# Retention with a squared-ReLU layer on one core: tail stores as single transfers, seven products for the last group, another formula for S2 and later places for four loads

## The chip, the cores and the metric

The kernel runs on one core of one Trainium2 chip. The time is the device time of one launch in microseconds (us). A profile is one execution under the hardware profiler; its span, from first to last instruction, is about 2 us shorter than the time. With a single core there is no second die to compare with.

## The reference, cut to what matters

Eight batches of 576 positions and eight heads go through causal retention, and the result (4608 tokens of 512) through two dense layers with a squared ReLU between them.

```python
def _attn_ref(q, k, v):                        # [8, 8, 576, 64] each
    scores = scale * np.matmul(q, k.transpose(0, 1, 3, 2))
    ...
    Dmat = np.where(rel >= 0, gamma[:, None, None] ** rel[None, :, :], 0.0)
    return np.matmul(scores * Dmat[None], v)

def _moe_ref(x, w_in, w_out):                  # [4608, 512], [512, 2048], [2048, 512]
    r = np.maximum(x @ w_in, 0.0)
    return (r * r) @ w_out
```

576 is 4 x 128 + 64. The work is cut into units of 128 tokens: 32 full ones, and four "tail" units, each made of the last 64 positions of two batches. Two units are a group.

## The kernel before

A small scheduler in the program knows a duration and a wished place for every instruction, and from these it fixes the order on each engine. TensorE computes the first layer of a group (ph), ScalarE takes relu (rl), ScalarE or VectorE squares it (gT), and TensorE computes the second layer (po). From a certain group on the second layer uses seven products of quarter size in Strassen's way (Winograd's form). They need four sums S1 to S4 of quarters of gT (tile gS, on VectorE), each made in two halves:

```python
        s3 = add_sum(2, base - 12, lambda h: G(0, 0, h), lambda h: G(1, 0, h), ALU.subtract, low)
        s1 = add_sum(0, base, lambda h: G(1, 0, h), lambda h: G(1, 1, h), ALU.add, ...)
        s2 = add_sum(1, base + 1, lambda h: Sx(0, h), lambda h: G(0, 0, h), ALU.subtract, lambda h: [s1[h]])
        s4 = add_sum(3, base + 4, lambda h: G(0, 1, h), lambda h: Sx(1, h), ALU.subtract, lambda h: [s2[h]])
        ...
        p6 = product(6, 8, "a", summed(1), wT[1], lambda h: [s2[h]], False, True, [c1])
```

Only the last group (a tail unit and a full unit) is excepted and uses the plain second layer; its last unit is cut into two halves of columns. The result goes out with one function. A tail unit's tile holds 64 rows of one batch and 64 of the next, which lie apart in DRAM, so it takes two transfers:

```python
    def store(u, o, lo=0, hi=DM):
        kind, b, c = units[u]
        eng = nc.scalar if group_of[u] == len(groups) - 1 else nc.sync
        if kind == "full":
            r0 = b * S + c * P
            eng.dma_start(out=out[r0:r0 + P, lo:hi], in_=o[:, lo:hi])
        else:
            for i in range(2):
                r0 = (b + i) * S + 512
                eng.dma_start(out=out[r0:r0 + 64, lo:hi], in_=o[i * 64:(i + 1) * 64, lo:hi])
```

All loads are issued by SyncE in a fixed sequence, and the scheduler has one figure for when each lands:

```python
    FIRST = ["k0", "q0", "v0", "k2", "q2", "w0", "v2", "w1", "w2", ..., "k4", "q4", "v4", ...]
    ...
        t = dma_task(0, 2.75, fn, acq=("wst",))          # weights
```

## Time and profile before

| | before |
|---|---|
| time, median of 3 runs | 298.6 us (298.57 to 298.71) |
| span of the profile | 296.6 us |
| last matmul ends | 293.46 us |
| last store is issued | 293.88 us, 2.7 us before the span's end |

The second is the end of the same kernel in stretches of 1 us. The columns are the stretch, its length, five engines' busy time, TensorE's clock, the DMA engines' busy share and GB/s.

```profile
293.00:294.00 1.00, 0.45 (x5) 0.15 (x2) 0.00 (x0) 0.37 (x1) 0.00 (x0) 1.00 0.42 141
294.00:295.00 1.00, 0.00 (x0) 0.00 (x0) 0.00 (x0) 0.00 (x0) 0.00 (x0) 1.00 0.25 86
295.00:296.00 1.00, 0.00 (x0) 0.00 (x0) 0.00 (x0) 0.00 (x0) 0.00 (x0) 1.00 0.14 45
```

Within 2 us of the last matmul the bytes are out. (The 0.14 of the last line is one short burst: in quarters of a microsecond it is 0.55 and then three times 0.00.) The third is SyncE's queue in the middle, by start, duration of the issue, and transfer: a tail store as two transfers, and the loads of a full unit behind it.

```profile
166.31 1.18 SPq L796 DMA_DIRECT2D out_dram<-o  x2
167.53 0.58 SPq L277 DMA_DIRECT2D k<-in_k_dram  x1
168.16 0.69 SPq L277 DMA_DIRECT2D q<-in_q_dram  x1
168.90 0.83 SPq L277 DMA_DIRECT2D v<-in_v_dram  x1
```

The issue of a load takes 0.6 to 0.8 us behind this store, and 0.4 to 0.9 us from here to 180. That is the yardstick for the kernel after.

### The profile page before, as it was taken

The page shows a single profiled execution, that of the slowest core. Times are in us where ns is not written, and L with a number is a line of the kernel's source. Part 1 is how long each engine was busy: PE and PEld are TensorE (multiplying, and loading weights), DVE is VectorE, ACT ScalarE, POOL GpSimd, SP SyncE. Part 2 cuts the span into 40 slices and gives each one's busy share as a digit, 9 for nine tenths or more (in the row PEclk, how much of TensorE's full clock was granted, in tenths as well). Part 3 has the DMA queues.
Part 4 walks back from the last instruction along what each step waited for, and adds up shares of the span by engine and source line. Part 5 has one row for each costly group of instructions (what it writes and reads, how often), then busy time and mean ns, then how long its engine had stood idle before and what let it go on. Part 6 is the DMA issues. An engine that isn't in the chain of part 4 may idle for free.

```text
span 296.6 us, 10048 instructions
## 1 busy us (share of the span) xinstructions
PE 286.1 (96%) x4320; PEld 233.5 (79%) x4320; DVE 196.2 (66%) x413; ACT 187.5 (63%) x354; POOL 93.9 (32%) x129
## 2 busy tenths in 40 slices
PE   8979999999989999999999999999999999999995
PEld 3558755688878888888788888788888888888874
DVE  4777469967495959593959596766786766462410
ACT  5257753474867676648576667756666666658861
POOL 4454384544232506062414142435141520000000
PEclk9999999999999999999999999999999999999999
DMA  7999998899999989999969698999898980101012
GB/s 205 326 373 385 361 270 220 207 202 180 200 148 216 195 195 169 212 196 199 180 163 160 157 190 206 206 201 205 142 215 140 219 133 32 73 3 71 2 71 73
DMA packets 139261, 54.14 MB, mean 183 GB/s; under 512 B 118096, under 2 KB 130640, under 8 KB 139216
## 3 DMA queue, kind: packets, MB, share of 16 engines
q1 hardware_dynamic: 138768, 52.97, 86.2%
q8 instruction: 34, 0.56, 0.8%
q10 hardware_dynamic: 448, 0.52, 0.6%
q14 instruction: 11, 0.09, 0.1%
HBM read 36.70 MB, written 9.44 MB: 156 GB/s over the span
## 4 chain that ended last, share of the span: by engine, by line
PE 64%; DVE 11%; ACT 10%; DMA 9%; issue 2%; POOL 2%; POOLq 0%
PE po L912 26%; PE ph L819 25%; DVE gS L890 5%; ACT rl L827 5%; ACT gT L837 4%; PE psO L337 4%; PE po L860 4%; DMA pair<-in_v_dram 3%; DMA wo<-in_moe_w_out_dram 3%; DMA pair<-in_k_dram 3%; PE warm L241 2%; DVE gT L839 2%; PE psc L337 1%; PE psS L337 1%; PE psT L412 1%
## 5 line engine op out<-in xcount | busy, mean ns | idle before, releaser
L819 PE MATMUL ph<-xT,w_in 128*128 128x256 f16 x1152 | 139.3, 273 | 0.0
L819 PEld LDWEIGHTS <-w_in 128*128 128x128 f16 x1152 | 111.2, 98 | 14.8 <-POOL w_in L316 0.3
L827 ACT ACTIVATE rl<-ph 128x512 f16<-128x512 f32 x144 | 84.1, 588 | 51.4 <-PE ph L819 48.9
L837 ACT ACTIVATE gT<-rl 128x512 f16<-128x512 f16 x112 | 70.6, 630 | 3.4
L890 DVE TENSOR_TENSOR gS<-gT 128x512 f16<-128x512 f16 x60 | 31.8, 531 | 40.3 <-ACT gT L837 39.7
L912 PEld LDWEIGHTS <-gS 128*128 128x128 f16 x480 | 45.6, 98 | 9.8 <-DVE gS L890 4.5
L912 PE MATMUL po<-wT,gS 128*128 128x256 f16 x360 | 49.2, 273 | 2.0 <-DVE gS L890 1.9
L361 POOL TENSOR_TENSOR v<-v,vdec_full 128x512 f16<-128x512 f32 x24 | 26.2, 1092 | 58.4 <-DMA v<-in_v_dram 51.0
L912 PEld LDWEIGHTS <-gT 128*128 128x128 f16 x360 | 34.7, 98 | 4.2
L912 PE MATMUL po<-w_out,gT 128*128 128x256 f16 x240 | 31.1, 273 | 0.0
L349 POOL CAST kq<-k 128x512 f16<-128x512 f32 x28 | 19.0, 677 | 36.9 <-DMA k<-in_k_dram 35.6
L839 DVE TENSOR_TENSOR gT<-rl 128x512 f16<-128x512 f16 x32 | 18.1, 568 | 13.8 <-ACT rl L827 13.4
L349 POOL CAST kq<-q 128x512 f16<-128x512 f32 x28 | 18.1, 647 | 23.3 <-DMA q<-in_q_dram 23.2
L860 PE MATMUL po<-w_out,gT 128*128 128x512 f16 (+1 forms) x112 | 22.6, 349 | 0.1
L925 ACT COPY u<-po 128x256 f32<-128x256 f32 x30 | 11.0, 367 | 15.5 <-PE po L912 15.4
L935 DVE TENSOR_TENSOR o<-po,u 128x256 f32<-128x256 f32 x30 | 12.6, 419 | 11.8 <-PE po L912 8.1
L698 DVE TENSOR_TENSOR xT<-psO,gam_full 128x512 f16<-128x512 f32 x28 | 18.4, 684 | 2.7 <-PE psO L337 2.5
L637 DVE TENSOR_TENSOR rT<-psc,mask 128x512 f16<-128x512 f32 x28 | 18.5, 681 | 1.4 <-PE psc L337 1.4
L890 DVE TENSOR_TENSOR gS<-gS,gT 128x512 f16<-128x512 f16 x30 | 16.3, 544 | 1.0
L860 PEld LDWEIGHTS <-gT 128*128 128x128 f16 x112 | 10.6, 98 | 7.9 <-issue 0.2
L912 PE MATMUL po<-wT,gT 128*128 128x256 f16 x120 | 15.8, 273 | 0.0
L890 DVE TENSOR_TENSOR gS<-gT,gS 128x512 f16<-128x512 f16 x30 | 15.1, 505 | 1.0
(78 smaller groups left out, 264.2 us busy)
## 6 DMA issues: line engine op xcount, KB each, us to landing
out_dram<-o SPq DMA_DIRECT2D x31, 256.0 KB, 3.1
k<-in_k_dram SPq DMA_DIRECT2D x24, 256.0 KB, 4.9
q<-in_q_dram SPq DMA_DIRECT2D x24, 256.0 KB, 4.9
v<-in_v_dram SPq DMA_DIRECT2D x24, 256.0 KB, 4.6
wi<-in_moe_w_in_dram SPq DMA_DIRECT2D x4, 1024.0 KB, 9.9
wo<-in_moe_w_out_dram SPq DMA_DIRECT2D x4, 1024.0 KB, 9.5
pair<-in_k_dram SPq DMA_DIRECT2D x4, 512.0 KB, 5.7
pair<-in_q_dram SPq DMA_DIRECT2D x4, 512.0 KB, 5.4
```

The source lines that it names most:

```text
L337: nc.tensor.matmul(out_, lhsT=lhsT, rhs=rhs, start=start, stop=True, skip_group_check=True, tile_position=(64 * row, 64 * col))
L349: op(out=out_.rearrange("p (n b a d) -> p n b a d", n=2, b=2, a=2), in_=in_.rearrange("p (n a b) d -> p n b a d", n=2, a=2))
L361: nc.gpsimd.tensor_tensor(out=t, in0=tile_of["v32", u], in1=vdec[kind].rearrange("p (h o) -> p h o", o=1).to_broadcast([P, H, D]), op=ALU. ...
L637: nc.vector.tensor_tensor(out=r, in0=tile_of["psc", g][:, :, cols(s)].rearrange("p a (n i) -> p a n i", i=64), in1=mask.rearrange("p (o r ...
L698: nc.vector.tensor_tensor(out=tile_of["x", g][:, :, s * P:(s + 1) * P].rearrange("p n (c i) -> p c n i", c=2), in0=tile_of["psO", g][:, :, ...
L819: nc.tensor.matmul(tile_of["ph", g, fb][:, j, :], lhsT=w_in16[:, m, fi * P:(fi + 1) * P], rhs=tile_of["x", g][:, m, :], start=(m == 0), st ...
L827: nc.scalar.activation(out=t, in_=tile_of["ph", g, fb], func=ACTF.Relu)
L837: nc.scalar.activation(out=t, in_=rl, func=ACTF.Square)
L839: nc.vector.tensor_tensor(out=t, in0=rl, in1=rl, op=ALU.mult)
L860: nc.tensor.matmul(tile_of["po", u, lo], lhsT=tile_of["g", g][:, fi, s * P:(s + 1) * P], rhs=w_out16[:, fi, lo:hi], start=(fi == 0), stop= ...
L890: nc.vector.tensor_tensor(out=Sx(k, h), in0=in0(h), in1=in1(h), op=op)
L912: nc.tensor.matmul(tile_of["pb", g, bank], lhsT=left(i), rhs=right[:, i, :], start=(start and i == 0), stop=(i == HF - 1), skip_group_chec ...
```

## The change

The change has four parts. A tail unit is stored with one transfer instead of two, so that the queue holds fewer issues. The last group also gets seven products, with its first layer spread between the products of the group before, so that TensorE has fewer columns to do. S2 is taken as A22 - S3 instead of S1 - A11 (the two are equal), so that it no longer waits for S1. And the scheduler is told that four loads (v2, w1, k4, q4) come later, so that it places what depends on them later.

```diff
+    SPREAD = 0.9
+    SQ_LATE = (1, 4, 6)
+    LAG = {"v2": 1.2, "w1": 1.3, "k4": 0.7, "q4": 0.5}
...
-        t = dma_task(0, 2.75, fn, acq=("wst",))
+        t = dma_task(0, 2.75, fn, acq=("wst",), after=2.1 + LAG.get(f"w{i}", 0.0))
...
-    def store(u, o, lo=0, hi=DM):
+    def store(u, o, lo=0, hi=DM, eng=nc.sync):
...
-            for i in range(2):
-                r0 = (b + i) * S + 512
-                eng.dma_start(out=out[r0:r0 + 64, lo:hi], in_=o[i * 64:(i + 1) * 64, lo:hi])
+            eng.dma_start(out=out.rearrange("(b s) m -> b s m", s=S)[b:b + 2, 512:576, lo:hi], in_=o[:, lo:hi])
...
-        base = us[0] * L
+        base = min(us) * L
+        def place(x):
+            return base + x if g < last_g else base - NF * n - 1 + SPREAD * x
...
-        if STRASSEN <= g < len(groups) - 1:
+        if STRASSEN <= g:
             add_strassen(g, us, base2, sq)
...
-        s1 = add_sum(0, base, lambda h: G(1, 0, h), lambda h: G(1, 1, h), ALU.add, ...)
-        s2 = add_sum(1, base + 1, lambda h: Sx(0, h), lambda h: G(0, 0, h), ALU.subtract, lambda h: [s1[h]])
+        s2 = add_sum(1, base - 4, lambda h: G(1, 1, h), lambda h: Sx(2, h), ALU.subtract, lambda h: high(h) + [s3[h]])
+        s1 = add_sum(0, base + 1, lambda h: G(1, 0, h), lambda h: G(1, 1, h), ALU.add, ...)
...
+        if g == last_g:
+            ...                       # other PSUM banks for products 3 and 4, additions on VectorE
         for u, ds in ((uA, [d11, c12]), (uB, [d22, d21])):
-            st = add("SP", -0.5, 0.7, lambda u=u: store(u, o_tile(u)), deps=ds, after=2.5)
+            if g < last_g: ...        # as before
+            else: ...                 # last group: one store per half, on SyncE or ScalarE
```

More of the change, by code (lines that the diff above doesn't have):

```diff
@@ L292, in fn @@
             nc.sync.dma_start(out=x, in_=(k, q, v)[n][b, :, c * P:(c + 2) * P, :].rearrange("h (p e) d -> p h (e d)", e=2))
-        loaded[name, u] = loaded[name, u + 1] = dma_task(0, 1.81 if loaded else 2.9, fn, acq=("wst",) if name != "q" else ())
+        loaded[name, u] = loaded[name, u + 1] = dma_task(0, 1.81 if loaded else 2.9, fn, acq=("wst",) if name != "q" else (),
+                                                         after=2.1 + LAG.get(name + str(u), 0.0))
     def add_weight(i):
@@ L784 @@
     wT_done = t1 + t2 + t3 + t4
-    def store(u, o, lo=0, hi=DM):
+    def store(u, o, lo=0, hi=DM, eng=nc.sync):
         kind, b, c = units[u]
-        eng = nc.scalar if group_of[u] == len(groups) - 1 else nc.sync
         if kind == "full":
@@ L820, in f @@
                                          rhs=tile_of["x", g][:, m, :], start=(m == 0), stop=(m == NP - 1))
-                f1.append(add("PE", base + (nf * fb + j) * n, 0.01 + 0.2133 * n, f,
+                f1.append(add("PE", place((nf * fb + j) * n), 0.01 + 0.2133 * n, f,
                               deps=[T["x", u] for u in us] + wcast_of(nf * fb + j) + f1[-1:],
@@ L827, in fr @@
                 nc.scalar.activation(out=t, in_=tile_of["ph", g, fb], func=ACTF.Relu)
-            on_act = n == 2 and g >= STRASSEN and fb in SQ_ACT
+            on_act = g >= STRASSEN and fb in (SQ_ACT if g < last_g - 1 else SQ_LATE)
             def fg(fb=fb, on_act=on_act):
@@ L839, in fg @@
                     nc.vector.tensor_tensor(out=t, in0=rl, in1=rl, op=ALU.mult)
-            r = add("ACT", base + 4 * fb + 4, 0.6, fr, deps=[f1[-1]], acq=("rl",))
+            r = add("ACT", place(4 * fb + 4), 0.6, fr, deps=[f1[-1]], acq=("rl",))
             sched.free("ff", [r])
-            sq.append(add("ACT" if on_act else "DVE", base + 4 * fb + 6, 0.63 if on_act else 0.45, fg, deps=[r] + sq[:1],
+            sq.append(add("ACT" if on_act else "DVE", place(4 * fb + 6), 0.63 if on_act else 0.45, fg, deps=[r] + sq[:1],
                           acq=() if fb else ("g",)))
@@ L852, in add_ff @@
             f2 = T["ff2"][-1:] if s == 0 else f2[-1:]
-            cuts = [(0, DM)] if u != groups[-1][-1] else [(0, HM), (HM, DM)]
-            for ci, (lo, hi) in enumerate(cuts):
-                for fi in range(NF):
-                    def f(fi=fi, s=s, u=u, lo=lo, hi=hi):
-                        if fi == 0:
-                            tile_of["po", u, lo] = ps_ff.tile([P, hi - lo], FP32, name="po", tag="ff")
-                        nc.tensor.matmul(tile_of["po", u, lo], lhsT=tile_of["g", g][:, fi, s * P:(s + 1) * P],
-                                         rhs=w_out16[:, fi, lo:hi], start=(fi == 0), stop=(fi == NF - 1))
-                    f2.append(add("PE", base2 + NF * s + fi / len(cuts) + 8 * ci, 0.0025 + 0.2135 / len(cuts), f,
-                                  deps=[sq[fi // nf]] + wcast[4 + fi // 4] + f2[-1:],
-                                  acq=("ff",) if fi == 0 else ()))
-                def fo(u=u, lo=lo, hi=hi):
-                    if lo == 0:
-                        tile_of["o", u] = o_pool.tile([P, DM], FP32, name="o", tag="o")
-                    nc.scalar.copy(out=tile_of["o", u][:, lo:hi], in_=tile_of["po", u, lo])
-                oc = add("ACT", end + 1, 0.12 + 0.47 / len(cuts), fo, deps=[f2[-1]], acq=() if lo else ("o",))
-                sched.free("ff", [oc])
-                st = add(*(("ACT", end + 1.1, 0.05) if g == len(groups) - 1 else ("SP", -0.5, 0.7)),
-                         lambda u=u, lo=lo, hi=hi: store(u, tile_of["o", u], lo, hi), deps=[oc], after=2.5)
@@ new lines, in add_ff, with f @@
+            for fi in range(NF):
+                def f(fi=fi, s=s, u=u):
+                    if fi == 0:
+                        tile_of["po", u] = ps_ff.tile([P, DM], FP32, name="po", tag="ff")
+                    nc.tensor.matmul(tile_of["po", u], lhsT=tile_of["g", g][:, fi, s * P:(s + 1) * P],
+                                     rhs=w_out16[:, fi, :], start=(fi == 0), stop=(fi == NF - 1))
+                f2.append(add("PE", base2 + NF * s + fi, 0.216, f, deps=[sq[fi // nf]] + wcast[4 + fi // 4] + f2[-1:],
+                              acq=("ff",) if fi == 0 else ()))
@@ L874, in add_ff, with fo @@
+            def fo(u=u):
+                tile_of["o", u] = o_pool.tile([P, DM], FP32, name="o", tag="o")
+                nc.scalar.copy(out=tile_of["o", u], in_=tile_of["po", u])
+            oc = add("ACT", end + 1, 0.59, fo, deps=[f2[-1]], acq=("o",))
+            sched.free("ff", [oc])
+            st = add("SP", -0.5, 0.7, lambda u=u: store(u, tile_of["o", u]), deps=[oc], after=2.5)
             sched.free("o", [st])
@@ L899, in add_strassen @@
         s3[0]["acq"] = ("wst",)
-        s1 = add_sum(0, base, lambda h: G(1, 0, h), lambda h: G(1, 1, h), ALU.add, lambda h: low(h) + high(h) + s3[:1])
-        s2 = add_sum(1, base + 1, lambda h: Sx(0, h), lambda h: G(0, 0, h), ALU.subtract, lambda h: [s1[h]])
+        s2 = add_sum(1, base - 4, lambda h: G(1, 1, h), lambda h: Sx(2, h), ALU.subtract, lambda h: high(h) + [s3[h]])
+        s1 = add_sum(0, base + 1, lambda h: G(1, 0, h), lambda h: G(1, 1, h), ALU.add, lambda h: low(h) + high(h) + s3[:1])
         s4 = add_sum(3, base + 4, lambda h: G(0, 1, h), lambda h: Sx(1, h), ALU.subtract, lambda h: [s2[h]])
@@ L949, in add_strassen, with f7, f12 @@
         c4 = on_act_copy("u4", "a", 21, [p5])
-        d22 = on_dve_add(uB, 1, "c", "u4", 22, [p7, c4], ("o",))
-        sched.free("u4", [d22])
-        p3 = product(3, 20, "a", summed(3), wB[1, 1], lambda h: [s4[h]], False, True, [c4])
-        def f12():
-            nc.scalar.copy(out=o_tile(uA)[:, HM:], in_=bank("a"))
-        c12 = add("ACT", base + 25, 0.37, f12, deps=[p3, d11])
-        sched.free("ff", [c12])
-        p4 = product(4, 24, "c", raw(1, 1), wT[3], high, False, True, [d22])
-        d21 = on_dve_add(uB, 0, "c", "u2", 29, [p4, d22])
-        sched.free("ff", [d21])
-        sched.free("u2", [d21])
+        if g == last_g:
+            def f7():
+                t = tile_of["p1", g] = u_pool.tile([P, HM], FP32, name="p1", tag="p1")
+                nc.vector.tensor_tensor(out=t, in0=bank("c"), in1=tile_of["u2", g], op=ALU.add)
+            d7 = add("DVE", base + 18, 0.42, f7, deps=[p7, c2], acq=("p1",))
+            sched.free("u2", [d7])
+            d22 = on_dve_add(uB, 1, "c", "u4", 22, [c4, d7])
+            sched.free("ff", [d22])
+            sched.free("ff", [c4])
+            p3 = product(3, 20, "d", summed(3), wB[1, 1], lambda h: [s4[h]], True, True, [])
+            p4 = product(4, 24, "e", raw(1, 1), wT[3], high, True, True, [])
+            c12 = on_dve_add(uA, 1, "d", "u4", 25, [p3, d22])
+            d21 = on_dve_add(uB, 0, "e", "p1", 29, [p4, d22])
+            d22["acq"] = ("o",)
+        else:
+            d22 = on_dve_add(uB, 1, "c", "u4", 22, [p7, c4], ("o",))
+            sched.free("u4", [d22])
+            p3 = product(3, 20, "a", summed(3), wB[1, 1], lambda h: [s4[h]], False, True, [c4])
+            def f12():
+                nc.scalar.copy(out=o_tile(uA)[:, HM:], in_=bank("a"))
+            c12 = add("ACT", base + 25, 0.37, f12, deps=[p3, d11])
+            sched.free("ff", [c12])
+            p4 = product(4, 24, "c", raw(1, 1), wT[3], high, False, True, [d22])
+            d21 = on_dve_add(uB, 0, "c", "u2", 29, [p4, d22])
+            sched.free("ff", [d21])
+            sched.free("u2", [d21])
         sched.free("wst", [p3])
@@ L965, in add_strassen @@
         for u, ds in ((uA, [d11, c12]), (uB, [d22, d21])):
-            st = add("SP", -0.5, 0.7, lambda u=u: store(u, o_tile(u)), deps=ds, after=2.5)
-            sched.free("o", [st])
+            if g < last_g:
+                st = [add("SP", -0.5, 0.7, lambda u=u: store(u, o_tile(u)), deps=ds, after=2.5)]
+            else:
+                st = []
+                for d in ds:
+                    lo = 0 if d in (d11, d21) else HM
+                    eng = ("ACT", base + 25.1, 0.05) if d in (c12, d22) else ("SP", -0.5, 0.05)
+                    st.append(add(*eng, lambda u=u, lo=lo, eng=eng: store(u, o_tile(u), lo, lo + HM,
+                                                                          nc.scalar if eng[0] == "ACT" else nc.sync),
+                                  deps=[d], after=2.5))
+            sched.free("o", st)
     for g in range(len(groups)):
```

## The prediction

> **What bounds the kernel now.** I first read the page's busy shares and its granted clock, then PE's waits, then the chain of waits, and last the timeline of the three places that the change touches: the first 60 us, one group of the middle, the last 25 us.
>
> ```profile
> PE 286.1 (96%) x4320; PEld 233.5 (79%) x4320; DVE 196.2 (66%) x413; ACT 187.5 (63%) x354; POOL 93.9 (32%) x129
> PEclk9999999999999999999999999999999999999999
> ```
>
> TensorE is busy for 286.1 of 296.6 us at full clock, so time comes off in two ways only: fewer matmul columns, or fewer of the 10.5 us in which PE stands still. 1.26 us of those lie before the first matmul and about 3.1 us after the last one. PE's waits name most of the rest:
>
> ```profile
> PE po L912 <- DVE gS L890: 1.9, 5, 0.8
> PE psS L337 <- POOL vx L393: 1.5, 1, 1.5
> ```
>
> The first line is the middle: the seven-product (Strassen) second layer waits for one of the sums on VectorE. Ends of matmuls are modelled, so I also took starts: a matmul of 256 columns starts every 0.109 us (48 pieces of po at the end: 6.96 us for 16 x 512 + 32 x 256 columns, 0.435 us per 1024). Wherever the next row starts later than its count times 0.109, PE lost time. In the eight groups where the second half of product 6 waits for S2 that excess is 0.93, 0.23, 0.49, 0.14, 0.67, 0.20, 0.32 and 0.32 us, together 3.3 us, against 1.9 in the waits view. The worst of them:
>
> ```profile
> 80.67 0.41 DVE L839 TENSOR_TENSOR gT<-rl 128x512 f16<-128x512 f16 x1
> 81.11 1.30 DVE L890 TENSOR_TENSOR gS<-gT 128x512 f16<-128x512 f16 x1
> 82.45 0.80 DVE L890 TENSOR_TENSOR gS<-gS,gT 128x512 f16<-128x512 f16 x1
> ...
> 81.94 0.60 PE L819 MATMUL ph<-xT,w_in 128*128 128x256 f16 x4
> 83.31 0.61 PE L912 MATMUL po<-wT,gS 128*128 128x256 f16 x4 [0.77 <-DVE gS L890]
> ```
>
> The last square of the group (gT) ends at 81.08. Then VectorE makes S1 (81.11, 1.30 us, normally 0.42) and from it S2 (82.45, 0.80 us). PE has started four ph matmuls at 81.94 and must wait until 83.31.
>
> The second wait, 1.5 us, is at the start: PE reaches the state sums psS at 18.05, but the decayed values come from a v load that lands at 17.9 and a product on GpSimd until 19.5. The end:
>
> ```profile
> 286.34 7.11 PE L860 MATMUL po<-w_out,gT 128*128 128x512 f16 x48
> ...
> 293.48 0.37 ACT L869 COPY o<-po 128x256 f32<-128x256 f32 x1 [1.19 <-PE po L860]
> 293.88 0.34 ACTq L792 DMA_DIRECT2D out_dram<-o  x1
> ```
>
> In the chain of waits everything from 254.91 to 293.46 is PE; then come one copy and one store, to 296.6. The last group is the only late one with the plain second layer.
>
> **What the Trainium skill says.** "TensorE: Matmul & The Clock Gate", Back-to-back issue gap, gives N/2.4 + 2.5 ns for one matmul in isolation, 109 ns for 256 columns and 216 for 512, though it gives shorter gaps for sustained streams. The trace agrees with the first form: 0.109 and about 0.217 us. So time is proportional to columns, and seven products for eight pay in full. "SBUF — State Buffer", SBUF: two separate sides, says that an operation of VectorE with two SBUF inputs and one of GpSimd lock each other out for a whole instruction. The sums have two SBUF inputs, and the trace fits: the slow sum at 81.11 lies beside a GpSimd v product from 81.10 to 82.14, and sums without a GpSimd neighbour take 0.42. "DMA: Bandwidth & Descriptors", Issuing engines are not separate DMA queues, says that all issuers share 16 engines and that a second issuer only saves issue time; the trace shows 0.53 to 0.60 us of issue for most halves of a tail store, 1.2 us for the pair on ScalarE at 290.6.
>
> **The change, part by part.**
>
> *Tail stores in one transfer.* One issue, by estimate as long as one half's (0.55 us), instead of two, four times. None is on the chain: the last one, at 290.61, has ended long before the last matmul. 0.0 us.
>
> *Seven products for the last group.* It removes 16 matmuls of 512 and 32 of 256 columns, 16384 columns, and adds 56 of 256, 14336. That is 2048 columns, or 8 x 0.109 = 0.87 us less PE; from the chain's 6.96 us to 56 x 0.109 = 6.10, so 0.86. It adds on VectorE eight sums (0.42) and five additions (0.42), and of the squares of the last two groups eight more move to VectorE, 8 x 0.43 = 3.4 us. VectorE is busy only 9.3 of the 20 us from 260 and 1.3 of the last 17, so all of this fits. The order of the instructions shows how the sums are hidden: the first layer of the last group is now spread between the products of the group before, with its last four ph matmuls just ahead of the last two of product 4. Counting from the end of those ph: relu 0.6, square 0.43, S2 0.42 and about 0.25 of handovers give 1.7 us; PE needs that half of S2 after 2 + 8 + 8 + 4 matmuls, 22 x 0.109 = 2.4 us. Slack 0.7 us, no new wait expected. The last step is an addition on VectorE (0.42) in place of a copy on ScalarE (0.37), +0.05, and the store before it is now 0.87 us ahead instead of 1.56, so they share the engines: I allow 0.1. Sum: -0.86 + 0.15 = -0.7 us.
>
> *S2 = A22 - S3.* The count of operations is the same. S2's second half now comes directly behind the last square instead of behind S1, so one sum earlier: 0.42 us, or 1.30 where GpSimd interferes, but the operation that follows the square then probably meets that interference itself. The scheduler has used the earlier S2, too: in most groups it puts four fewer ph matmuls ahead of product 6's second half. So the waits don't go altogether. From the start of product 1 in each group I set when PE wants that half (0.109 per matmul, about 0.74 for scores and sums) against when the square ends plus the first sum after it as in the trace before. Group 3: wanted 3.8, there at 2.94 + 1.30 = 4.27, 0.5 left of 0.93. The group at 184.87: the square ends at 3.76, S2 at 4.2 to 4.5, wanted at 3.5: 0.8 for 0.67. The one at 214.80: 3.74 against 3.5, 0.25 for 0.32. Two others keep 0.1 to 0.15, the rest nothing. 3.3 us become about 1.8: -1.5 us.
>
> *Loads with late packets placed later.* Nothing lands earlier by this: the DMA engines are full to 40 us, and the model only learns that v2, w1, k4 and q4 come later. On PE, eight ph and one warming matmul move ahead of psS, so about 1.1 of the 1.5 us of waiting are filled. But the next ph need the second w_in block, cast by 21.87 in the trace before, when the old order arrived at 21.92; PE then waits there for about 1.06. After that the new order takes the blocks of the first group before those of the second, and reaches the fourth w_in block at 26.5; its cast was done at 27.3 to 27.5. Up to 0.9 is lost again, and 0.2 before the first w_out block (29.8). Against this stand 0.3 at the kx transposes (41.0) and 0.2 at 48.9 which go, and eight ph matmuls that now fill the wait for kqT. My replay comes to +0.2 us; as its start times are uncertain by more than that and the part was aimed at these very waits, I take 0.0, with 0.7 either way.
>
> Sum: -0.7 - 1.5 + 0.0 = -2.2 us, so 298.6 becomes 296.4 us.
>
> **The rivals.** First, the waits only move: VectorE still delivers the last square late, as at 184.87 where its xT and state chain comes first, and S2 keeps its 3.3 us. For it: the new order leaves fewer ph between; against it: in eight of the fifteen groups S2 would be ready 0.3 us or more before it is wanted. Then -0.7, 297.9 us. Second, all waits for S2 go, and the start gains what was meant, 1.0 us: -0.7 - 3.3 - 1.0, 293.6 us. For it: the lags look as if read from a trace; against it: weights that no order brings earlier. Third, the end doesn't hide its sums: eight squares more on VectorE, and only four PSUM banks for three products in flight and the spread ph. A missed half of S2 or a bank costs 0.5 to 1 us and eats the 0.86: 297.2 us. Fourth, loads bind: the DMA row of the page is at 9 until 240 us. Against it: the SP queue itself waits for stores (35.4 us for the o additions), so loads are paced by compute, and PE never waits for a transpose in the middle.
>
> **Range and chances.** Tail -0.9 to 0.0, S2 -3.0 to -0.3, start -0.8 to +0.8; they're independent, so 294.9 to 297.6 us. 2% is 6.0 us. All that the change can reach is 6.5: the 3.3 at S2, 0.86 of matmuls, and 2.3 of waits at the start (1.5, 0.3 twice, 0.2). So faster by 2% would need nearly all of it; slower by 2% would need a new wait of 6 us, for which nothing speaks.
>
> **What would show it.** Right: PE's wait on gS below 1.9 us and the excess at product 6 about halved; the final run of po being 56 matmuls of 256 in about 6.1 us without a gap; the first po at about the same time, within 0.7 us of 30.1, and the wait for vx shorter with a new one for w_in. Wrong: a gap inside the last 56 matmuls, po of the first group well before 29.8 us, or new PE waits for relu, squares or banks from 270 us on.

## More of the kernel before

Beside the lines that the prediction shows, three views are needed later. The first is the row of the DMA engines on the page: 40 slices of 7.4 us, each digit the mean busy share of 16 engines in tenths.

```profile
DMA  7999998899999989999969698999898980101012
```

The last slices are 1, 0, 1 and 2: the stores at the end leave the engines mostly idle.

## The result, and the profile after

The kernel after takes 302.35 us (median of 6 runs, 302.1 to 302.95). The kernel before, run beside it, had 298.65. A ratio here is the mean time of one kernel's runs over the mean of the other's in the same rounds, so it isn't quite the ratio of these medians: 1.0123, with a 95% interval of 1.0095 to 1.0151. That is within 2%, but slower by 3.7 us where 2.2 us less was expected, and outside the range.

The page of the kernel after, the same three rows:

```profile
PE 284.2 (95%) x4328; PEld 234.5 (78%) x4328; DVE 197.8 (66%) x434; ACT 183.2 (61%) x346; POOL 94.9 (32%) x129
PEclk9999999999999999999999999999999999999997
DMA  7999999899998998999999689998999930110022
```

TensorE is busy 1.9 us less than before, and its clock is full in every slice but the last. The extra time isn't TensorE's. PE's waits, three lines of the view:

```profile
PE psc L341 <- DMA kqT<-kq: 1.7, 1, 1.7
PE ph L823 <- POOL w_in L320: 1.2, 2, 0.8
PE psS L341 <- POOL vx L397: 0.3, 1, 0.3
```

The wait for the sums (gS) is gone from the view. The wait for vx has shrunk from 1.5 to 0.3, and one for w_in has come, both as foreseen. A wait for the transposed keys and queries (kqT) is new. The timeline of the group that the prediction showed as the worst (group 3):

```profile
80.53 0.42 DVE L843 TENSOR_TENSOR gT<-rl 128x512 f16<-128x512 f16 x1 [0.54 <-ACT rl L831]
80.99 0.43 DVE L888 TENSOR_TENSOR gS<-gT,gS 128x512 f16<-128x512 f16 x1
81.34 1.27 DVE L888 TENSOR_TENSOR gS<-gT 128x512 f16<-128x512 f16 x1
...
82.41 0.60 PE L910 MATMUL po<-wT,gS 128*128 128x256 f16 x4
```

S2 (inputs gT and gS) now comes directly behind the square and takes 0.43 us; S1 has the slow place behind it. Product 6 goes on at 82.41 without a wait, where it had waited for 0.77.

The end is another matter. First the last matmuls in the chain of waits, then the stores and the last addition in the timeline:

```profile
286.40 6.35 PE po L910 x58
```

```profile
290.66 0.55 SPq L796 DMA_DIRECT2D out_dram<-o  x1
...
292.36 1.13 ACTq L796 DMA_DIRECT2D out_dram<-o  x1
292.77 0.42 DVE L933 TENSOR_TENSOR o<-po,p 128x256 f32<-128x256 f32 x1 [0.45 <-PE po L910]
293.23 0.34 SPq L794 DMA_DIRECT2D out_dram<-o  x1
```

The last matmul ends at 292.75, 0.7 us earlier than before, and the last store is issued at 293.23. But the span ends at 300.6, 7.4 us after that issue instead of 2.7. Stores on line 796 are the tail unit's two halves (128 rows of 256 numbers, 128 KB each), those on line 794 the full unit's. The end in stretches of 1 us, columns as before:

```profile
294.00:295.00 1.00, 0.00 (x0) 0.00 (x0) 0.00 (x0) 0.00 (x0) 0.00 (x0) 1.00 0.88 237
...
296.00:297.00 1.00, 0.00 (x0) 0.00 (x0) 0.00 (x0) 0.00 (x0) 0.00 (x0) 1.00 0.13 38
297.00:298.00 1.00, 0.00 (x0) 0.00 (x0) 0.00 (x0) 0.00 (x0) 0.00 (x0) 0.77 0.13 41
298.00:299.00 1.00, 0.00 (x0) 0.00 (x0) 0.00 (x0) 0.00 (x0) 0.00 (x0) 0.50 0.13 46
```

In the stretch from 294 most of the full unit's halves goes out, at a share of 0.88. Then three microseconds follow at a share of 0.13 and about 42 GB/s, 125 KB in all. 0.13 x 16 is two engines' worth: a merged tail store moves on two of 16 engines. By estimate the two halves need 256 KB / 42 GB/s = 6.2 us, and that is the end of the kernel. (The falling clock at the end has no matmul to slow.)

A share could also come from many engines that are each busy for a short part of the time. The packet records of the kept trace, which no view prints, settle it. From 295.6 to 298.9 two packets of 1 KB are in flight for 85% of the time and three for nearly all of the rest; in the kernel with two transfers per tail store (a_two below) up to 19 are, and a packet takes as long (46 and 47 ns in the median). There are also records of 4 bytes at the end of transfers: 18 on each of the two queues here, 48 on each in a_two. That is 16 for a full unit's half and 2 for a merged tail half, against three times 16. The last two, at 298.9 and 299.3 on ScalarE's queue, are those of the tail unit's second half.

The same shape can be seen in the middle. SyncE's queue of the kernel after, where a merged tail store of 256 KB goes out at 164.87:

```profile
164.87 0.61 SPq L796 DMA_DIRECT2D out_dram<-o  x1
165.53 1.37 SPq L280 DMA_DIRECT2D q<-in_q_dram  x1
166.95 2.99 SPq L280 DMA_DIRECT2D v<-in_v_dram  x1
169.98 3.74 SPq L283 DMA_DIRECT2D k<-in_k_dram  x2
```

The issues behind it take 1.4, 3.0 and 1.9 us each, against 0.4 to 0.9 before. In the packet records this store's two final records come only at 172.8, and in the 2 us from 172 the DMA share is only 0.19:

```profile
172.00:174.00 2.00, 2.00 (x21) 1.80 (x19) 1.47 (x5) 1.39 (x3) 0.00 (x0) 1.00 0.19 50
```

The transpose of kqT stands behind these loads in the queue, and TensorE waits 1.67 us for it, until 179.5.

With the starts of product 1 as marks, the 4.0 us by which the span grew can be laid out by stretch. Groups are counted from 0, and the last group is number 17:

| stretch | before | after | difference |
|---|---|---|---|
| start to group 2 | 63.42 | 63.71 | +0.29 |
| group 2 to 9 | 106.07 | 104.55 | -1.52 |
| group 9 to 10 (with the wait for kqT) | 15.38 | 18.05 | +2.67 |
| group 10 to 15 | 74.24 | 72.92 | -1.32 |
| group 15 to the last matmul's end | 34.35 | 33.52 | -0.83 |
| after the last matmul | 3.14 | 7.85 | +4.71 |
| sum | 296.6 | 300.6 | +4.0 |

Of the +2.67 us 1.67 are the wait for kqT and 0.71 a later one for a square (gT). The trace thus names two costs, both, it seems, of the part that I had put at 0.0 us, and three gains, together 3.7 us where 2.2 had been expected.

### The profile page after: what moved, and what is told of

Same layout as the page of the kernel before. It is cut to its first block, busy times and chain, and to the rows that moved or that the text cites. A ratio compares the mean times of both kernels' runs of the same rounds, so it can differ in the third digit from the quotient of the medians.

```text
span 300.6 us, 10099 instructions
## 1 busy us (share of the span) xinstructions
PE 284.2 (95%) x4328; PEld 234.5 (78%) x4328; DVE 197.8 (66%) x434; ACT 183.2 (61%) x346; POOL 94.9 (32%) x129
## 4 chain that ended last, share of the span: by engine, by line
PE 77%; DMA 9%; SPq 3%; DVE 3%; ACT 2%; issue 1%; POOL 1%; DVEq 0%; POOLq 0%
PE ph L823 35%; PE po L910 29%; PE po L861 5%; PE psO L341 4%; DMA pair<-in_v_dram 3%; DMA wo<-in_moe_w_out_dram 3%; DMA pair<-in_q_dram 2%; PE psc L341 2%; SPq L283 2%; SPq L280 1%; DMA kqT<-kq 1%; PE psS L341 1%; ACT rl L831 1%; ACT gT L841 1%; PE psT L416 1%
## 5 line engine op out<-in xcount | busy, mean ns | idle before, releaser
L841 ACT ACTIVATE gT<-rl 128x512 f16<-128x512 f16 x104 | 65.6, 631 | 3.0
L910 PEld LDWEIGHTS <-gS 128*128 128x128 f16 x512 | 49.4, 98 | 6.4 <-DVE gS L888 0.5
L910 PE MATMUL po<-wT,gS 128*128 128x256 f16 x384 | 52.4, 273 | 0.0
L888 DVE TENSOR_TENSOR gS<-gT,gS 128x512 f16<-128x512 f16 x64 | 33.3, 522 | 21.3 <-ACT gT L841 20.7
L888 DVE TENSOR_TENSOR gS<-gT 128x512 f16<-128x512 f16 x64 | 30.5, 476 | 21.5 <-ACT gT L841 21.4
L910 PEld LDWEIGHTS <-gT 128*128 128x128 f16 x384 | 37.2, 98 | 5.8 <-issue 1.4
L910 PE MATMUL po<-w_out,gT 128*128 128x256 f16 x256 | 33.5, 273 | 0.7 <-ACT gT L841 0.7
L910 PE MATMUL po<-w_out,gS 128*128 128x256 f16 x128 | 16.6, 273 | 0.0
L861 PE MATMUL po<-w_out,gT 128*128 128x512 f16 x64 | 15.6, 379 | 0.2 <-POOL w_out L320 0.2
L670 DVE TENSOR_TENSOR R<-stmp,dec 128x256 f16<-128x256 f32 x24 | 13.7, 572 | 0.7
```

The source lines that it names most:

```text
L841: nc.scalar.activation(out=t, in_=rl, func=ACTF.Square)
L861: nc.tensor.matmul(tile_of["po", u], lhsT=tile_of["g", g][:, fi, s * P:(s + 1) * P], rhs=w_out16[:, fi, :], start=(fi == 0), stop=(fi == N ...
L888: nc.vector.tensor_tensor(out=Sx(k, h), in0=in0(h), in1=in1(h), op=op)
L910: nc.tensor.matmul(tile_of["pb", g, bank], lhsT=left(i), rhs=right[:, i, :], start=(start and i == 0), stop=(i == HF - 1), skip_group_chec ...
```

## The experiments

The theory, A: the merged tail store has an outermost dimension of two (the two batches), and this confines it to two engines. At the end it is on the path; in the middle it holds up the loads behind it. Rival B: the new order in the last group and the four later loads cost the time, and the store only happens to be the last thing. Rival C: what is slow is one large transfer as such, in place of two small ones.

In the table, "us" is (ratio - 1) x 298.6, so the difference to the kernel before on the same chip and in the same rounds; different calls ran on different chips, and this is the safer figure across them.

| run | median | ratio to before (95%) | us |
|---|---|---|---|
| after | 302.35 | 1.0123 (1.0095 to 1.0151) | +3.7 |
| a_two | 297.61 | 0.9971 (0.9951 to 0.9991) | -0.9 |
| a_mid_merged | 297.50 | 0.9970 (0.9934 to 1.0007) | -0.9 |
| a_end_merged | 301.58 | 1.0111 (1.0086 to 1.0135) | +3.3 |
| a_cols | 305.55 | 1.0236 (1.0211 to 1.0260) | +7.0 |
| b_merged | 304.00 | 1.0177 (1.0137 to 1.0217) | +5.3 |
| b_s2_lag | 298.19 | 0.9997 (0.9974 to 1.0021) | -0.1 |
| a_two_olds2 | 298.48 | 1.0009 (0.9987 to 1.0032) | +0.3 |
| a_two_nolag | 296.46 | 0.9947 (0.9922 to 0.9972) | -1.6 |
| a_two_lagkq | 296.01 | 0.9910 (0.9885 to 0.9936) | -2.7 |
| a_two_nolag_q | 295.57 | 0.9905 (0.9874 to 0.9937) | -2.8 |
| a_lagkq_q | 295.44 | 0.9900 (0.9866 to 0.9933) | -3.0 |

Names that begin with a_ start from the kernel after, with b_ from the kernel before. All results were correct.

### a_two: the kernel after with two transfers per tail store again

```diff
-            eng.dma_start(out=out.rearrange("(b s) m -> b s m", s=S)[b:b + 2, 512:576, lo:hi], in_=o[:, lo:hi])
+            for i in range(2):
+                r0 = (b + i) * S + 512
+                eng.dma_start(out=out[r0:r0 + 64, lo:hi], in_=o[i * 64:(i + 1) * 64, lo:hi])
```

> The changed kernel with each tail store as two transfers of 64 rows again, all else kept, instruction order included. Theory A (the merged store, whose outermost dimension has size 2, runs on 2 of the 16 DMA engines): the end shrinks from 7.4 us after the last addition to about 2.8, and the 2.7 us that group 10 loses to the late kqT go; from the last matmul at 292.7 that gives 292.7 - 2.7 + 0.5 + 2.8 = 293.3 us of span, about 295.2 us of time. Rival B (the new order of the last group and of the loads costs the time, the stores are innocent): 301 to 302.5.

It took 297.61 us (297.2 to 298.24): 4.5 us of the kernel after are gone with this one line (+3.7 to -0.9; the intervals are far apart). The expectation was 2.4 us too low: it carried the gains of the trace after over at face value, but in the trace of a_two the start and the middle give 1.5 us less, and the end took 3.3 us instead of 2.8. The last store, and the end in stretches:

```profile
292.12 0.34 SPq L794 DMA_DIRECT2D out_dram<-o  x1
```

```profile
293.00:294.00 1.00, 0.00 (x0) 0.00 (x0) 0.00 (x0) 0.00 (x0) 0.00 (x0) 1.00 0.72 197
294.00:295.00 1.00, 0.00 (x0) 0.00 (x0) 0.00 (x0) 0.00 (x0) 0.00 (x0) 1.00 0.00 0
```

All bytes are out at 294, and the span ends at 295.4, 3.3 us after the last issue. Rival B falls: its parts are all still in this kernel, and it is faster than the kernel before.

### a_mid_merged and a_end_merged: merged in one place only

```diff
-            eng.dma_start(out=out.rearrange(...)[b:b + 2, 512:576, lo:hi], in_=o[:, lo:hi])
+            if group_of[u] < len(groups) - 1:        # a_end_merged: == len(groups) - 1
+                eng.dma_start(out=out.rearrange(...)[b:b + 2, 512:576, lo:hi], in_=o[:, lo:hi])
+            else:
+                for i in range(2):
+                    ...                              # two transfers as before
```

> Merged tail stores only in the groups before the last, two transfers at the end. Theory A: keeps the loss in the middle alone, about 2.7 us over the kernel with two transfers everywhere, so about 297.9. If the merged stores in the middle are hidden and the late kqT has another cause (order of the queue): the same whether merged or not, the 2.7 us also appear with two transfers everywhere, and this run equals it.

> Merged tail stores only in the last group. Theory A: keeps the slow end alone, about 4.6 us over the kernel with two transfers everywhere: about 299.7, with DMA at about 0.13 of 16 engines for the last 5 us. Rival B: no different from two transfers everywhere.

Merging at the end alone gives 301.58 us, 4.2 us more than a_two (+3.3 to -0.9). Its end has the same plateau at two engines:

```profile
296.00:297.00 1.00, 0.00 (x0) 0.00 (x0) 0.00 (x0) 0.00 (x0) 0.00 (x0) 0.82 0.14 42
```

The last issue is at 292.37 and the span ends at 299.7, 7.3 us later. So the end accounts for nearly all of the 4.5 us.

Merging in the middle alone gives 297.50 us, no different from a_two. Yet its trace has a wait for kqT, of 1.0 us. The two kernels differ in the stores of the middle alone, and so the two traces show what a merged one does there. Behind it the issue of a v load takes 3.92 us (0.69 in a_two), and from 168 to 170 the share is that of two engines, with only packets of 2 KB in flight, the size of this store's rows (0.90 and 207 GB/s in a_two):

```profile
168.00:170.00 2.00, 2.00 (x49) 1.63 (x50) 1.27 (x4) 1.97 (x5) 0.00 (x0) 1.00 0.13 44
```

Every one of the four profiled kernels with merged stores in the middle has this wait (1.7, 1.0, 2.0 and 1.9 us), and the waits of the other kernels list none for a kqT transfer. The six runs of a_mid_merged fall in two clusters, 296.3 to 296.6 and 298.5 to 299.6. I had expected up to 2.7 us here, and that was a miss: the traces show a new wait, but the times don't show a cost of it (0.0 us by this pair, 0.4 by after against a_end_merged). The profiled execution is the fastest of the six, and in it the late starts at product 6 (counted below) are 0 us, against 1.1 in a_two, so in that execution another wait is smaller by as much. Two of the three upper runs show a granted clock of 0.992 and 0.993, the other four runs 1.000. Whether the wait costs time in some executions only stays open.

### a_cols: two transfers, each with an outermost dimension of two

```diff
+            mid = (lo + hi) // 2
+            for l, h in ((lo, mid), (mid, hi)):
-            eng.dma_start(out=out.rearrange(...)[b:b + 2, 512:576, lo:hi], in_=o[:, lo:hi])
+                eng.dma_start(out=out.rearrange(...)[b:b + 2, 512:576, l:h], in_=o[:, l:h])
```

> Each tail store as two transfers again, but split by columns, so that each still has 2 as its outermost dimension. Theory A: nothing is gained over the changed kernel, 302 to 304 us. Rival C (one large transfer is slow because it is one; what counts is the number of transfers or their size): recovers as the split by rows does, 295 to 297.

This one has the number and the sizes of a_two's transfers, but not their shape: it cuts the columns, so each piece still spans both batches. It took 305.55 us, 7.9 us more than a_two and 3.4 more than the kernel after. The end:

```profile
298.00:299.00 1.00, 0.00 (x0) 0.00 (x0) 0.00 (x0) 0.00 (x0) 0.00 (x0) 0.50 0.13 31
```

Again 0.13 of the engines, and with rows half as long 31 GB/s here and up to 42 three microseconds later. Rival C falls: with the number and the size of a_two's transfers the end is at least as slow as with one transfer, so it is the outermost dimension that decides. What the shorter rows add isn't separated here.

### b_merged: the kernel before with merged tail stores only

The edit is the store's line of the change, nothing else.

> The kernel before with merged tail stores alone. Theory A: the tail store of the last group, 256 KB from 290.6 on at the 41 GB/s that two engines gave in the changed kernel, needs 6.4 us and ends near 297.8, behind the last store of 128 rows; span near 298.5, time near 300.5, plus up to 2.7 in the middle. Rival B (the order of the last group is what makes it slow): 298.6 as before.

304.00 us, 5.3 us over the kernel before, so the part costs even more by itself, and more than I gave it. The last two stores in its timeline:

```profile
293.42 1.13 ACTq L794 DMA_DIRECT2D out_dram<-o  x1
296.70 0.34 ACTq L792 DMA_DIRECT2D out_dram<-o  x1
```

Two terms are in it. The wait for kqT (1.9 us in its trace) pushed everything back; from group 9 to 10 this trace takes 19.04 us where the kernel before takes 15.38. The wait is only half of these 3.7 us. After it the granted clock fell, to 0.50 from 182 to 184, and 16 matmuls from 181.13 on took 3.39 us, where they took 1.91 before. And from the last issue to the span's end it is 6.2 us instead of 2.7. In the packet records the merged store (rows of 2 KB) ends at 300.8, and the full unit's halves behind it on the same queue (1 KB) at 301.5. In this kernel both terms are on the path, as far as one trace tells.

### a_two_olds2 and b_s2_lag: what S2 and the seven products are worth

a_two_olds2 is a_two with the sums S1 and S2 as before the change. b_s2_lag is the kernel before with the new S2 and the LAG table, and without the seven products for the last group or the merged stores.

> Two transfers per tail store, seven parts, loads placed later, but S2 from S1 and A11 as before. If the new S2 is worth the 1.5 us that the prediction gave it (the trace gains 1.7 between groups 2 and 15): 299.1 to 299.4. If the waits had only moved: as with the new S2, 297.6.

> The kernel before with the new S2 and the later loads alone: plain last group, its stores from ScalarE, two transfers. If seven parts for the last group are worth 0.86 us of PE less some of the end of the stores: 298.0 to 298.3, that is 0.4 to 0.7 slower than with seven parts. If the end gives all of it back: 297.6.

a_two_olds2 took 298.48 us, 0.9 more than a_two in medians and 1.1 by ratios; the two intervals just touch. Its waits show where:

```profile
PE po L912 <- DVE gS L890: 2.0, 5, 0.5
```

The late starts at product 6, counted as in the prediction but over all groups, are 3.1 us with the old S2 and 1.1 in a_two (3.4 before, 0.2 after). They vary from trace to trace: 2.2 to 3.4 us in the three kernels with the old S2, 0 to 1.6 in the ten with the new one. So the new S2 takes away about 2 us of that wait in this pair. The two profiled executions do differ by 2.2 us in their times, but they are nearly the slowest of the one kernel and the fastest of the other; of the medians' difference they say little. Other short waits come and go in the same groups, such as those for the additions on VectorE (1.0 us in b_s2_lag, none listed before).

b_s2_lag took 298.19 us, in the middle of what was expected. The seven products are then worth 0.6 us in medians and 0.8 by ratios, though the intervals of a_two and b_s2_lag overlap.

### a_two_nolag and a_two_lagkq: what the later loads are worth

```diff
-    LAG = {"v2": 1.2, "w1": 1.3, "k4": 0.7, "q4": 0.5}
+    LAG = {}                                   # a_two_nolag
+    LAG = {"k4": 0.7, "q4": 0.5}               # a_two_lagkq
```

> Two transfers per tail store, seven parts, new S2, but no later placing of loads. The part itself: in the trace of the kernel with two transfers the start of product 1 in group 2 lies 0.75 us behind the kernel before (0.3 in the changed kernel), with waits for w_in (0.8 and 0.4) in place of the one for vx. If the later placing loses time: 0.3 to 0.8 us faster than with it, 296.8 to 297.3. If it gains what it was meant for: slower by 0.5 to 1.5, 298 to 299.

> Two transfers per tail store, seven parts, new S2; of the later placing only that of k4 and q4, not of v2 and w1. Theory: the later placing loses by v2 and w1, which bring the fourth w_in block to the front too early (waits for w_in of 0.8 and 0.4 us in the traces that have it). Then this equals the kernel without any later placing, about 296.5, with a wait for vx of about 1.3 and none for w_in. If k4 and q4 are what loses: as with all of it, 297.6.

Without the table the time is 296.46 us, 0.7 us (ratios) to 1.1 us (medians) below a_two: the table as a whole seems to cost, though these intervals overlap. With the two entries for k4 and q4 alone it is 296.01 us, 1.8 us below a_two by ratios, and the intervals don't overlap. So the entries for v2 and w1 are what costs. Whether those for k4 and q4 gain isn't settled; the intervals of a_two_nolag and a_two_lagkq overlap. In PE's waits of a_two_lagkq the wait for w_in is gone and the one for vx is back:

```profile
PE psS L341 <- POOL vx L397: 1.4, 1, 1.4
```

By the order of the matmuls, the change had filled this wait with some taken from later, and had then to wait for w_in.

### a_two_nolag_q and a_lagkq_q: the last tail store on two queues

Two transfers share 16 engines anyway, but their issues stand one behind the other: 1.18 us for the pair on ScalarE. Here SyncE issues the first one of each last tail store.

```diff
+                e = nc.sync if i == 0 and group_of[u] == len(groups) - 1 else eng
-                eng.dma_start(out=out[r0:r0 + 64, lo:hi], in_=o[i * 64:(i + 1) * 64, lo:hi])
+                e.dma_start(out=out[r0:r0 + 64, lo:hi], in_=o[i * 64:(i + 1) * 64, lo:hi])
```

> The best so far (two transfers per tail store, seven parts, new S2, no later placing), with the first half of the last tail store issued by SyncE and only the second by ScalarE. Theory: the last store waits on the DMA engines behind the second of those halves, which ScalarE issues 0.6 us late; 0.3 us off the end, about 296.2. If the end is bound by the last store's own latency: 296.5, no change.

> Both together: k4 and q4 placed later, v2 and w1 not, and the last tail store issued by SyncE and ScalarE. If the two add up (the second took 0.5 off the ratio's 0.9947): 0.987 to 0.990 of the kernel before, 295.0 to 295.8. If the range of the middle, about 1 us between executions, covers it: as each of them alone, 0.991.

a_two_nolag_q took 295.57 us. Its last issue is at 290.73 and the span ends at 293.6, so the end is 2.9 us instead of 3.3. The ratio fell by more (0.9947 to 0.9905), but the intervals overlap, and I can't assign the rest. a_lagkq_q, with both steps, took 295.44 us (294.21 to 296.49): ratio 0.9900, 3.0 us below the kernel before and 6.9 us below the kernel after in medians. It is the lowest of all and beats both, though it isn't clearly better than either step alone.

## Why the prediction was wrong

**What bounds the kernel: right.** TensorE at full clock sets the time as long as it works. After the last matmul nothing of TensorE counts, and there I didn't look closely enough.

**Tail stores in one transfer, "0.0 us": this is the step that failed.** As I put it, "None is on the chain: the last one, at 290.61, has ended long before the last matmul." I counted issues and took for granted that one transfer of 128 KB moves as fast as two of 64 KB. Nor was the old one's margin long: its packets ran from 291.8 to 293.2 in the trace before, and the last matmul ended at 293.46. Measured, the part costs 4.5 us (after against a_two), 4.2 of them at the end alone. The Trainium skill, "DMA: Bandwidth & Descriptors", Why a DMA increments its semaphore by 16 and not by 1, says that the number of engines is the largest up to 16 that divides the slowest dimension, other than one of size 1, of both sides, and gives as an instance 16 for a tile of 128 partitions. For the new store that dimension is 2 in DRAM, so two engines; for the two old ones it is 64, so 16. The trace agrees: a share of 0.13 of 16 engines and about 42 GB/s in after, against 0.72 and 197 in a_two, and 2 final records for a merged store against 16. I had cited another section of the same page and not asked how many engines the new shape would get. The line of the diff carried it: a rearranged output with the batch outermost.

The prediction also took the wrong store for the deciding one. The full unit's half, issued last at 293.23, had at least 14 of its 16 final records by 295.4, and its queue's last records came at 297.6; the tail unit's second half, issued at 292.36, was the last to land, at 299.3.

**The saving in issues didn't count either.** The estimate of 0.55 us held on SyncE (against 1.12 for the pair); on ScalarE the merged half took 1.13 us, the pair 1.18. Neither is on the path.

**Seven products for the last group, -0.7: right, as far as the noise lets one say.** 0.6 to 0.8 us by a_two against b_s2_lag, with intervals that overlap; in the traces the stretch from group 15 to the last matmul is 0.83 us shorter. The last 56 matmuls run without a gap (with the last two of the group before 58, in 6.35 us), and no wait for sums or banks came. One term of it was mis-sized: for the end I allowed 0.15 more, and in a_two the time after the last matmul is about 0.6 us more than before (3.76 against 3.14), probably since more of the stores now fall together.

**S2, -1.5: direction and mechanism right, the size less so.** I expected 1.8 of the 3.3 us to remain at product 6; 0 to 1.6 did, by trace. In the time 0.9 to 1.1 us arrive (a_two against a_two_olds2).

**Loads placed later, 0.0 with 0.7 either way: low by 0.7 to 1.1, if the overlapping intervals of a_two and a_two_nolag are taken at their middles.** The replay itself was good. It foresaw new waits of about 1.06, up to 0.9 and 0.2 us; the trace has 0.77, 0.46 and 0.19. But I overruled its result of +0.2, in part because the change "was aimed at these very waits". The purpose of a change is no evidence of its effect.

**The sum.** With measured terms by ratios: -0.8 (seven products) - 1.1 (S2) + 0.7 (loads) + 4.5 (stores) = +3.3 us, against +3.7 measured. Without the stores the sum is -1.2, and a_two has -0.9. So the range was missed through the store alone: a_two at 297.61 lies at its upper edge. (That edge was too low by its own terms: independent spans of 0.7, 1.2 and 0.8 us above -2.2 give 1.6 us, so 298.0.)

**The rivals.** The sentence against a slower kernel, "slower by 2% would need a new wait of 6 us, for which nothing speaks", was where the miss could have been seen. The end alone brought 4.7 us. None of the four rivals concerned the transfers' own duration.

## What to carry to other kernels

When a transfer is merged or its access pattern rearranged, look first at the outermost dimension on both sides: putting the two batches outermost took this store from 16 engines to two, and the number of transfers told nothing here. After the last matmul every microsecond of a store is on the path, so the end of a kernel is read by the DMA share (0.13 for two engines) as much as by its issues. A part's purpose shouldn't overrule a replay that says otherwise.

## What the Trainium skill lacked or had wrong

- "DMA: Bandwidth & Descriptors", Why a DMA increments its semaphore by 16 and not by 1, has the rule on which all hangs, and the runs bear it out; what it lacks there is a rate for few engines. The page's Specifications have one figure, about 27 GiB/s per engine, which for two would be 58 GB/s by estimate. Two engines moved less here: 33 to 48 GB/s with rows of 1 KB (after, a_end_merged) and 31 to 42 GB/s with rows of 512 bytes (a_cols). A packet took 84 ns for 2 KB, 46 ns for 1 KB and 27 ns for 512 bytes.
- The same section doesn't say what such a transfer does to those behind it on its queue. In after, load issues that followed a merged store of 256 KB took 1.4 to 3.0 us instead of 0.4 to 0.9, the DMA share fell to 0.19, and TensorE waited 1.7 us for a transpose behind them. The pair a_mid_merged and a_two, which differ in these stores alone, shows the same: 3.92 against 0.69 us for one issue, and a wait of 1.0 us against none, in one trace each. No loss of time was measured for it in that pair.
- "TensorE: Matmul & The Clock Gate", Back-to-back issue gap, gives about 131 ns per matmul of 512 columns in a sustained stream. No stream here shows that: the kernel before had 216 to 217 ns, and 109 for 256 columns, which fit the formula that this section gives for a matmul in isolation.
